# First loads of an attention-and-rational-FFN kernel: S2 leads ScalarE's queue, the first keys go in two halves over two queues, and the written-out order is replaced

## The chip, the cores and the metric

One core of a Trainium2 chip runs the whole kernel. The metric is the device time of one launch in microseconds; the median of three runs before the change is 265.93 us (265.91 to 265.98). Differences are told as time after over time before.

## What is computed

Two parts follow each other. The first is attention with polynomial sketch features: for each of 4 batches and 4 heads, 1088 rows of q and k (32 wide) are multiplied by two small matrices S1 and S2 (8 x 32 each), and the 8 x 8 products of the two results are the 64 features of a row. Keys' features are summed against v (and against ones, for the denominator); a query's output is its features times that sum, divided by the denominator. The second part is a feed-forward layer whose activation is a ratio of polynomials.

```python
def phi(x):
    a = np.einsum('rd,bhsd->bhsr', S1, x)
    b = np.einsum('rd,bhsd->bhsr', S2, x)
    return np.einsum('bhsi,bhsj->bhsij', a, b).reshape(*x.shape[:-1], r * r)
q_p, k_p = (phi(q), phi(k))
kv = np.einsum('bhsf,bhsd->bhfd', k_p, v)
z = np.sum(k_p, axis=2)
num = np.einsum('bhsf,bhfd->bhsd', q_p, kv)
den = np.einsum('bhsf,bhf->bhs', q_p, z)[..., None] + 1e-06
...
h = x @ w_in                       # x: 4352 x 128, w_in: 128 x 2048
P = a[0] + a[1] * h + a[2] * h2 + a[3] * h3
Q = 1.0 + np.abs(b[0]) * np.abs(h) + np.abs(b[1]) * h2
g = P / (Q + 1e-06)
return (g @ w_out).astype(np.float32)
```

S1, S2, the four numbers a and the two numbers b are inputs like the rest, in DRAM at launch.

## The kernel before

**The order is written out by hand.** The kernel lists its work as steps: `step(engine, ..., fn, ...)` appends one, in the order of the source, and only notes which buffers it uses. Step number n of that list is emitted at position `PLACE[n]`. Each engine runs its own steps in that order and waits, by semaphores, for whatever a step needs; nothing overtakes on an engine or on its DMA queue. The numbers for cost, rank and slack that the calls carry (among them `GET_SLACK` and `S_SLACK`) are not used when the kernel is emitted. `ON_ACT` lists the steps that may run on either of two engines and are given to ScalarE; the rest of those go to VectorE. `FILLS` gives positions ahead of which TensorE runs multiplications of a zero tile (L321), so many each; they compute nothing that is used. `FILL = 1` adds one at the very start.

**The loads.** `dma(...)` issues one transfer, from SyncE's queue (SP) or from ScalarE's (ACT). All lines of it are L268. At the start SP issues S1, S2, the first 256 columns of q of batch 0 (`q0_a`), v of batch 0 in two parts (`load_v`, by partitions 0 to 63 and 64 to 127), then half of w_out, the rest of q0 (`q0_b`), the keys of batch 1, the other half of w_out and the first half of w_in. ScalarE issues the keys of batch 0 in one transfer of 544 KB (`load_k`, 128 partitions of 4352 bytes), then b, loads its activation table, and issues a. S1 and S2 land in 8 rows each of one tile, `s_raw`.

**The start.** VectorE copies `s_raw` four times side by side into `s_rep` (L352). TensorE transposes that (L349), and VectorE multiplies it with masks into `S12` (L355, for keys) and two tiles `SAB` (L362, for queries); GpSimd copies it once more for later queries. Keys of batch 0: VectorE transposes them in 32 x 32 blocks into `kT` (L415, L417), in two pieces, tiles 0 to 3 and 4 to 8. In five parts (`K0_PARTS`: tile 0, tiles 1 to 3, 4 and 5, 6 and 7, 8) TensorE makes the sketches (L435), ScalarE copies one half (L440), VectorE multiplies the halves into features `k_p` (L443) and TensorE multiplies them with v (L454). ScalarE copies the sum into `kvz` (L473). Queries: block transposes (L498), two sketches (L520), a copy on ScalarE (L528 or L525), the product on VectorE (L535 or L532), then the multiplication with `kvz` (L589), the division (L598, L602, L605), a transpose on TensorE (L611) and a copy into `xT` (L618). Later groups of queries go through DRAM: a smaller sketch (L548), a copy (L553), two transfers out (`put`), three back (`get`), a product (L556).

**w_out.** The kernel needs w_out in bfloat16, five times: as it is and scaled with each of a's four numbers; each is made in two halves from the raw load (L391, L393 on ScalarE, L395, L397 on VectorE). Six of these ten steps are on ScalarE.

**The feed-forward part** runs in 29 units. A unit is up to six blocks of 512 rows by 128 columns of the hidden layer (the first four and the last ones are smaller). `hidden` multiplies (L691), ScalarE copies to bfloat16 (L695), VectorE and ScalarE make the ratio in passes: the absolute value (L706), b's polynomial (L711 or L713, then L716), its reciprocal as Ln and Exp on ScalarE (L719, L722), powers of h times that reciprocal (L726 to L752), and `gather` multiplies the results with the copies of w_out (L787). The string `MODES` has one digit a unit. A mode tells how a's polynomial is shared out: in mode 4 the powers go to TensorE one by one, four multiplications a block; in mode 3 a pass a3*h + a2 is made on VectorE or ScalarE (L726 or L728) and three multiplications a block remain; in mode 2 two. Finished columns are transposed by VectorE (L799) and written out (L811).

Of the kernel before, what the change touches and what calls it, by code (L numbers as in the profile page):

```python
# [20 lines left out]
def kernel(  # L21
# [103 lines left out]
    def d_four(n, ptr):  # L125
# [20 lines left out]
    GET_SLACK = 1.2  # L146
    S_SLACK = (0.0, 1.0)
# [5 lines left out]
    MODES = '43242333333243333233444244424'  # L153
# [60 lines left out]
    )  # L214
    ON_ACT = (
        25, 26, 29, 31, 32, 33, 328, 342, 344, 379, 454, 478, 502, 535, 612, 636, 669, 688, 693, 744, 878,
        889, 914, 932, 951, 953, 960,
    )
    FILLS = {7: 15, 22: 4, 70: 1, 77: 1}
    NW = 5 if '4' in MODES else 3  # L220


# [643 lines left out]
```

## Time and profile before

| what | value |
|---|---|
| median of 3 runs | 265.93 us (265.91 to 265.98) |
| the profiled execution, time and span | 265.84 us, 264.1 us |
| granted clock of TensorE | 1.00 |
| VectorE's first instruction | 4.34 us after the span's start |
| ScalarE's first instruction after its table load | 6.18 us |
| first hidden matmul (L691) | 16.53 us |
| last instruction that computes (VectorE, L799) | 260.24 us, 0.45 us long |
| bytes moved by DMA | 20.13 MB, mean 76 GB/s |

The span runs from the first to the last recorded instruction; the time is that of the launch and is 1.8 us longer. The costliest lines are L691 (127.2 us of TensorE, 320 matmuls), L787 (97.8 us of TensorE, 480), the copies L695 (69.4 us of ScalarE), Ln and Exp (65.5 and 65.4 us of ScalarE) and the two products L716 and L731 (40.4 us of VectorE each). In the lists that follow, a row of a timeline has the start, the time taken, the engine (ACTq and SPq are the queues that issue DMAs), the line, the operation with output and input, and the count; in brackets stands the idle time before it and what ended it. A row of waits has the engine and the work that waited, what it waited for, the total in us, how often and the longest.

### The profile page before, as it was taken

Reading aid. Unit: us, or ns where it says so; the run is one execution under the profiler, and the core shown is the slowest. Engines: PE = TensorE matmul, PEld = TensorE weight load, DVE = VectorE, ACT = ScalarE, POOL = GpSimd, SP = SyncE. Lnnn points to the kernel's source line nnn. Section 1 sums busy time; section 2 is a strip of 40 time slices with the busy share of each in tenths; the row PEclk is TensorE's granted clock in tenths of the full one; section 3 lists DMA queues with packets and bytes.
Section 4 is the critical chain, followed back from the end, with each engine's and each line's share of the span. In section 5 each row is a group of like instructions: output and inputs, shape, how many; then the busy total and the mean of one; then the engine's idle time right before and its main releaser. Section 6 shows DMA issues by size and latency. Waiting matters only on the chain.

```text
span 264.1 us, 4201 instructions
## 1 busy us (share of the span) xinstructions
PE 254.8 (96%) x1641; PEld 141.1 (53%) x1659; DVE 252.4 (96%) x293; ACT 248.5 (94%) x209; POOL 2.7 (1%) x25
## 2 busy tenths in 40 slices
PE   8999999999999999999999999999999999999994
PEld 5767646554544654454444554444444466565683
DVE  3889999999999999999999999999999999999994
ACT  2779999999999999999999999999999999999991
POOL 4000000000000000000000000000000000000000
PEclk9999999999999999999999999999999999999999
DMA  7969344800425347005102530300010110030032
GB/s 199 338 193 241 79 134 128 242 32 0 97 70 178 93 132 163 4 7 129 34 2 80 104 87 21 55 0 0 0 22 2 25 18 0 0 46 0 0 55 40
DMA packets 29063, 20.13 MB, mean 76 GB/s; under 512 B 19316, under 2 KB 24948, under 8 KB 29044
## 3 DMA queue, kind: packets, MB, share of 16 engines
q1 hardware_dynamic: 28352, 19.24, 29.2%
q10 hardware_dynamic: 692, 0.62, 0.8%
q8 instruction: 13, 0.21, 0.4%
q14 instruction: 6, 0.05, 0.1%
HBM read 16.65 MB, written 3.21 MB: 75 GB/s over the span
## 4 chain that ended last, share of the span: by engine, by line
ACT 51%; PE 30%; DVE 10%; issue 8%; POOL 0%; ACTq 0%; POOLq 0%
PE h_ps L691 14%; ACT ln L719 13%; ACT t L722 13%; ACT t L695 11%; PE out_ps L787 7%; ACT t L728 6%; ACT t L713 3%; DVE t L734 2%; DVE t L737 2%; PE att_ps L589 1%; DVE t L731 1%; PE att_ps L548 1%; DVE t L716 1%; PE att_ps L321 1%; PE att_ps L435 1%
## 5 line engine op out<-in xcount | busy, mean ns | idle before, releaser
L691 PE MATMUL h_ps<-xT,w_in_sb 128*128 128x512 f32 (+1 forms) x320 | 127.2, 534 | 1.2 <-ACT xT L618 0.7
L787 PE MATMUL out_ps<-t,w_out 128*128 128x512 bf16 (+1 forms) x480 | 97.8, 344 | 1.9 <-issue 1.1
L691 PEld LDWEIGHTS h_ps<-xT,w_in_sb 128*128 128x128 f32 x320 | 58.8, 190 | 45.4 <-issue 33.3
L787 PEld LDWEIGHTS <-w_out 128*128 128x128 bf16 x498 | 47.2, 98 | 49.5 <-issue 17.9
L695 ACT CAST t<-h_ps 128x1024 bf16<-128x1024 f32 (+1 forms) x69 | 69.4, 1053 | 0.5 <-PE h_ps L691 0.4
L719 ACT ACTIVATE ln<-t 128x3072 f32<-128x3072 bf16 (+4 forms) x29 | 65.5, 2257 | 0.3 <-DVE t L716 0.2
L722 ACT ACTIVATE t<-ln 128x3072 bf16<-128x3072 f32 (+4 forms) x29 | 65.4, 2254 | 0.2
L731 DVE TENSOR_TENSOR t<-t,t 128x3072 bf16<-128x3072 bf16 (+4 forms) x29 | 40.4, 1397 | 0.0
L716 DVE TENSOR_TENSOR t<-t,t 128x3072 bf16<-128x3072 bf16 (+4 forms) x29 | 40.4, 1392 | 0.0
L728 ACT ACTIVATE t<-t,a_sb 128x3072 bf16<-128x3072 bf16 (+2 forms) x13 | 33.3, 2574 | 0.4 <-PE out_ps L787 0.4
L734 DVE TENSOR_TENSOR t<-t,t 128x3072 bf16<-128x3072 bf16 (+3 forms) x23 | 32.7, 1425 | 0.1
L706 DVE TENSOR_SCALAR t<-t 128x3072 uint16<-128x3072 uint16 (+4 forms) x29 | 22.4, 773 | 0.6 <-ACT t L695 0.4
L711 DVE TENSOR_SCALAR t<-t,b_abs 128x3072 bf16<-128x3072 bf16 (+3 forms) x24 | 22.3, 928 | 0.0
L737 DVE TENSOR_TENSOR t<-t,t 128x3072 bf16<-128x3072 bf16 (+1 forms) x13 | 21.6, 1661 | 0.0
L589 PEld LDWEIGHTS att_ps<-kvz,a_all 128*64 128x64 f32 x288 | 9.9, 137 | 4.2 <-issue 2.3
L589 PE MATMUL att_ps<-kvz,a_all 128*64 128x66 f32 x288 | 11.3, 225 | 0.0
L752 DVE TENSOR_TENSOR t<-t,t 128x1024 bf16<-128x1024 bf16 (+3 forms) x10 | 11.2, 1124 | 0.0
L556 DVE TENSOR_TENSOR a_all<-a_all,b_all 128x768 f32<-128x768 f32 (+2 forms) x11 | 9.6, 871 | 0.0
L713 ACT ACTIVATE t<-t,b_abs 128x2048 bf16<-128x2048 bf16 (+3 forms) x5 | 9.0, 1809 | 0.1
L443 DVE TENSOR_TENSOR k_p<-att_ps,b_sk 128x768 f32<-128x768 f32 x9 | 8.5, 949 | 0.0
L454 PEld LDWEIGHTS att_ps<-v_sb,k_p 128*64 128x64 f32 x216 | 6.8, 138 | 2.1 <-issue 1.4
L740 DVE TENSOR_TENSOR t<-t,t 128x3072 bf16<-128x3072 bf16 (+3 forms) x6 | 7.7, 1282 | 0.0
(75 smaller groups left out, 145.9 us busy)
## 6 DMA issues: line engine op xcount, KB each, us to landing
a_all<-sk_d SPq DMA_DIRECT2D x6, 384.0 KB
b_all<-sk_d SPq DMA_DIRECT2D x12, 192.0 KB
kq<-in_k_dram SPq DMA_DIRECT2D x3, 544.0 KB
kq<-in_q_dram SPq DMA_DIRECT2D x3, 544.0 KB
a_all<-sk_d SPq DMA_DIRECT2D x4, 320.0 KB
b_all<-sk_d SPq DMA_DIRECT2D x8, 160.0 KB
v_sb<-in_v_dram SPq DMA_DIRECT2D x4, 288.0 KB
v_sb<-in_v_dram SPq DMA_DIRECT2D x4, 256.0 KB
```

The costliest lines, as they stand in the source:

```text
L589: nc.tensor.matmul(nd.t[x:x + 64, o:o + 2 * KW], lhsT=(av(c)[:, o0 + x:o0 + x + 64] if how == "direct" else q_p.t[:, c * n + o0 + x:c * n ...
L691: nc.tensor.matmul(h.t[:, cols[x] - cols[x0]:cols[x + 1] - cols[x0]], lhsT=w_in_sb[:, f * 128:(f + 1) * 128], rhs=xT[:, xpos(t0):xpos(t0) ...
L695: nc.scalar.copy(out=hh.t[:, cols[x0]:cols[x1]], in_=h.t[:, 0:cols[x1] - cols[x0]])
L706: nc.vector.tensor_scalar(out=u.t[:, :n].bitcast(U16), in0=hh.t[:, :n].bitcast(U16), scalar1=0x7FFF, scalar2=None, op0=AX.bitwise_and)
L716: nc.vector.tensor_mul(out=y.t[:, :n], in0=w.t[:, :n], in1=u.t[:, :n])
L719: nc.scalar.activation(out=ln.t[:, :n], in_=y.t[:, :n], func=ACT.Ln, bias=1.0 + 1e-6)
L722: nc.scalar.activation(out=r.t[:, :n], in_=ln.t[:, :n], func=ACT.Exp, scale=-1.0)
L728: nc.scalar.activation(out=p.t[:, :n], in_=hh.t[:, :n], func=ACT.Identity, scale=a3, bias=a2)
L731: nc.vector.tensor_mul(out=s.t[:, :n], in0=hh.t[:, :n], in1=r.t[:, :n])
L734: nc.vector.tensor_mul(out=(hh if mode == 3 else p).t[:, :n], in0=hh.t[:, :n], in1=s.t[:, :n])
L737: nc.vector.tensor_mul(out=hh.t[:, :n], in0=p.t[:, :n], in1=hh.t[:, :n])
L787: nc.tensor.matmul(o[0].t[:, :bl[x][1]], lhsT=w_sb[y_][:, bl[x][2], :], rhs=src.t[:, cols[x]:cols[x + 1]], start=(o[1] == 1), stop=(o[1] = ...
```

## The change

Four things change in the code.

1. S2 is issued by ScalarE, as the first of its queue, rather than by SyncE behind S1.
2. The keys of batch 0 are two transfers: partitions 0 to 63 by ScalarE behind S2, partitions 64 to 127 by SyncE behind S1.
3. The last unit (256 rows by 128 columns) goes from mode 4 to mode 3. That takes one of its four matmuls L787 away, and adds one pass of 256 columns a partition, given to ScalarE (step 966 of `ON_ACT`).
4. `PLACE`, `ON_ACT` and `FILLS` are new. There is one step more (977). The two numbers for slack have no part in what is emitted.

The head of each list, read from the two tables (numbers in brackets are warming matmuls in front):

| | before | after |
|---|---|---|
| SP queue | S1, S2, q0_a, v, v, w_out 2nd half, q0_b, keys of batch 1, w_out 1st half, w_in 1st half | S1, keys 64-127, q0_a, v, v, w_out 2nd half, q0_b, w_out 1st half, keys of batch 1, w_in 1st half |
| ACT queue | keys, b, table, a | S2, keys 0-63, b, a, table |
| VectorE | s_rep, kT of tiles 0-3, S12, SAB, qT, SAB, kT of tiles 4-8, features of tile 0, 1-3, query product, features 4-5, 6-7, 8 | s_rep, SAB, S12, SAB, kT of tiles 0-3, qT, kT of tiles 4-8, features of tile 0, 1-3, 4-5, query product, features 6-7, 8 |
| TensorE | (1+15) L349, (4) L435 of tile 0, 1-3, L377, L520, L520, L435 of 4-5, 6-7, L454 of tile 0, 1-3, L435 of 8, L454 of 4-5, 6-7, 8 | (1+9) L349, (8) L435 of tiles 1-3, tile 0, L520, L435 of 4-5, L520, L435 of 8, L454 of tile 0, L435 of 6-7, L377, L454 of 1-3, 4-5, 6-7, 8 |
| ScalarE, from its fifth copy L440 to L473 | a part of w_out ahead of it, one behind it | two parts of w_out behind it |

Of the w_out steps, ScalarE had the second halves of the copies 0, 2 and 3, the first half of copy 1 and both of copy 4; it now has both of 0 and 2 and the second of 1 and 4. In the rest of the kernel the steps of every engine keep their engine and mostly their neighbourhood, but 312 of TensorE's 354 have another rank than before, 193 of VectorE's 286 and 182 of ScalarE's 209.

```diff
     FILL = 1
     LATE = 6.96
     Q0B_RANK = -194.15
-    GET_SLACK = 1.2
-    S_SLACK = (0.0, 1.0)
+    GET_SLACK = 1.1
+    S_SLACK = (0.0, 0.0)
     V_SLACK = 0.99
     GAP = 0.2
     START = 4.9
     Q0_PRE = -151.2
     K1_RANK = 0.47
-    MODES = '43242333333243333233444244424'
+    MODES = '43242333333243333233444244423'
     FIRST_PER = 4
     LAST_PER = (8, 8, 8, 4, 3, 1)
     K0_PARTS = ((0, 1), (1, 4), (4, 6), (6, 8), (8, 9))
@@ -163,60 +163,60 @@
     PERS = (6,)
     N_T = 16
     PLACE = (
-        0, 3, 1, 8, 4, 5, 10, 2, 9, 18, 13, 71, 16, 17, 11, 6, 7, 14, 19, 21, 15, 29, 33, 30, 80, 46, 91,
-        66, 83, 58, 111, 43, 90, 101, 12, 24, 22, 23, 25, 38, 26, 27, 28, 39, 36, 40, 42, 48, 37, 41, 47,
...
+        1, 0, 3, 7, 6, 8, 9, 10, 4, 5, 27, 20, 65, 26, 21, 11, 2, 12, 14, 13, 16, 15, 42, 43, 60, 97, 57,
+        63, 46, 78, 45, 93, 103, 72, 79, 17, 25, 22, 28, 29, 37, 18, 19, 30, 47, 31, 32, 33, 48, 38, 39, 41,
...
     )
     ON_ACT = (
-        25, 26, 29, 31, 32, 33, 328, 342, 344, 379, 454, 478, 502, 535, 612, 636, 669, 688, 693, 744, 878,
-        889, 914, 932, 951, 953, 960,
+        25, 26, 28, 29, 30, 34, 329, 343, 345, 380, 455, 479, 503, 536, 613, 637, 670, 689, 694, 745, 879,
+        890, 915, 933, 952, 954, 961, 966,
     )
-    FILLS = {7: 15, 22: 4, 70: 1, 77: 1}
+    FILLS = {12: 9, 18: 8, 76: 1, 80: 1}
     NW = 5 if '4' in MODES else 3
 
 
@@ -263,10 +263,11 @@
 
     k0, q0, v0 = Buf("kq"), Buf("kq"), Buf("v_sb")
 
-    def dma(out_, in_, rank, mbytes, after=(), uses=(), eng=SP, early=0.0, rate=300, cost=0.46, slack=0.3, behind=None):
+    def dma(out_, in_, rank, mbytes, after=(), uses=(), eng=SP, early=0.0, rate=300, cost=0.46, slack=0.3, behind=None, name="go"):
         def go():
             (nc.sync if eng == SP else nc.scalar).dma_start(out=out_() if callable(out_) else out_,
                                                             in_=in_() if callable(in_) else in_)
+        go.__name__ = name
         return step(eng, cost, go, rank, after=after, uses=uses, land=mbytes * 1e3 / rate, early=early,
                     slack=slack, behind=behind)
 
@@ -288,11 +289,12 @@
         return dma(s_raw[i * R:(i + 1) * R], s_in, rank, 0.001, eng=eng, cost=0.4, slack=S_SLACK[i], behind=behind)
 
     s_l = [load_s(0, -206, SP)]
-    s_l.append(load_s(1, -205.9, SP, behind=s_l[0]))
+    s_l.append(load_s(1, -208, ACTE))
     FIRST = 256
-    k0_l = load_k(0, k0, -207, slack=0.15, rate=420, eng=ACTE)
+    k0_l = [dma(lambda x=x: k0.t[x:x + 64], flat(k, 0)[x:x + 64], -207 + 0.01 * x, 0.279, (), [k0], rate=420, slack=0.15,
+                eng=(ACTE, SP)[x // 64], behind=s_l[1 - x // 64], name=("go", "half")[x // 64]) for x in (0, 64)]
     table = step(ACTE, 1.3, lambda: nc.scalar.preload_act_table_set("natural_log_exp_and_others"), -205, behind=k0_l[0])
-    q0_a = dma(lambda: q0.t[:, 0:FIRST], flat(q, 0)[:, 0:FIRST], -203.8, 0.131, (), [q0], rate=350, slack=0.2, behind=s_l[1])
+    q0_a = dma(lambda: q0.t[:, 0:FIRST], flat(q, 0)[:, 0:FIRST], -203.8, 0.131, (), [q0], rate=350, slack=0.2, behind=k0_l[1])
     v0_l = load_v(0, v0, -203.7, slack=0.4, rates=(340, 205), behind=q0_a)
     ab_in = []
     for c, w, x in ((4, 2, moe_b), (0, 4, moe_a)):

```

Line numbers from here on are those of the kernel before; after the change, lines from L268 on stand one or two further down.

92 rows, old and new, of the table PLACE are left out of this document.

## The prediction

> **What bounds the kernel now.** I read the busy table of the page first, then busy time by stretch, then the waits of the first 28 us, then the start in order of time.
>
> ```profile
> PE 254.8 (96%) x1641; PEld 141.1 (53%) x1659; DVE 252.4 (96%) x293; ACT 248.5 (94%) x209; POOL 2.7 (1%) x25
> ```
>
> ```profile
> 12.00:16.00 4.00, 3.38 (x43) 1.94 (x41) 3.00 (x7) 2.61 (x8) 0.00 (x0) 1.00 0.71 202
> 16.00:20.00 4.00, 4.00 (x33) 3.47 (x30) 3.56 (x13) 3.62 (x6) 0.00 (x0) 1.00 0.73 230
> 20.00:250.00 230.00, 227.04 (x1349) 119.77 (x1366) 228.73 (x238) 229.07 (x176) 0.00 (x0) 1.00 0.26 64
> ```
>
> Columns of the second fence: stretch, its length, busy us of TensorE, weight loads, VectorE, ScalarE, GpSimd; granted clock, DMA share, GB/s. From 20 to 250 us three engines are busy at once: VectorE is idle 1.27 us, ScalarE 0.93 us, TensorE 2.96 us. No single engine can be relieved there; an order can only lose or save that little, and the start (idle VectorE, ScalarE) is where time lies.
>
> ```profile
> DVE s_rep L352 <- DMA s_raw<-in_S_dram: 4.3, 1, 4.3
> ACT b_sk L440 <- PE h_ps L435: 3.2, 2, 3.1
> DVE a_all L535 <- PE att_ps L520: 0.5, 1, 0.5
> ```
>
> ```profile
> 0.73 0.39 ACTq L268 DMA_DIRECT2D kq<-in_k_dram  x1
> 0.73 0.74 SPq L268 DMA_DIRECT2D s_raw<-in_S_dram  x2
> 4.34 0.21 DVE L352 COPY s_rep<-s_raw 16x128 f32<-16x128 f32 x1 [4.34 <-DMA s_raw<-in_S_dram]
> 4.49 0.41 SPq L268 DMA_DIRECT2D ln<-in_moe_w_out_dram  x1
> 4.49 0.77 DVE L415 STREAM_TRANSPOSE kT<-kq 128x256 f32<-128x256 f32 x2
> 5.19 0.19 DVE L355 TENSOR_TENSOR S<-att_ps,mask 128x64 f32<-128x64 f32 x1
> 5.30 0.28 DVE L362 TENSOR_TENSOR SAB<-att_ps,mask 128x128 f32<-128x128 f32 x1
> 5.50 0.43 DVE L498 STREAM_TRANSPOSE qT<-kq 128x256 f32<-128x256 f32 x1
> 5.84 0.25 DVE L362 TENSOR_TENSOR SAB<-att_ps,mask 128x128 f32<-128x128 f32 x1
> 6.02 0.75 DVE L415 STREAM_TRANSPOSE kT<-kq 128x256 f32<-128x256 f32 x2
> 11.92 0.43 ACT L473 COPY kvz<-out_ps 64x66 f32<-64x66 f32 x2
> 16.53 1.99 PE L691 MATMUL h_ps<-xT,w_in_sb 128*128 128x256 f32 x8
> ```
>
> Here: start, us, engine, work. VectorE waits 4.34 us for the two little matrices. The trace's packet records say why: S1's eight packets run at 1.68 to 1.76 us, S2's at 3.40 to 3.66, behind the keys' 128 packets (from 1.79; 0.17 us each once running; the last ends at 4.11). S1's semaphore is full at 2.10 us, S2's at 4.25, the keys' at 4.47.
>
> **S2 first on ScalarE's queue.** It leaves at 0.73 us like S1, with nothing in front, so I take S1's 2.10 us for it. s_rep then runs at 2.2. TensorE's warming matmuls (L321) ahead of the transpose L349 fall from 16 to 10, 0.213 us apart from 1.29: they end near 3.3. From L349 to S12 it is 0.48 us (4.70 to 5.19), so the three mask products run from 3.8 to 4.4, before the keys. Their room behind the keys was 0.11 + 0.20 + 0.18 us, start to start (5.19 to 5.30, 5.30 to 5.50, 5.84 to 6.02): **-0.49 us** of VectorE. s_rep itself gives nothing: its end was the keys' landing anyway.
>
> **Keys in two halves.** Both leave second on their queues, near 1.15 us (S2's old issue was at 1.19), not at 0.73: 0.39 to 0.46 us late. S1 and S2 bring 16 packets of 0.013 us, nothing. The halves need the same 128 packets on the same engines, which in the old load were full from 2.5 us. Bounds for the landing: 4.47 (two issuers fill the 16 engines at once; before, the first 0.5 us had them 3 of 16 busy) to 4.47 + 0.39 = 4.86. I take 4.75, nearer the late end as the engines, not the queue, were full: **+0.28 us** (0 to 0.39). The transposes need all partitions, so both halves count. The SP queue gets a 64-row issue in S2's place, so q0's and v's issues stay near 1.5 and 1.9; on ScalarE's queue b, a and the table load (1.28 us) follow, done by 4 us, before its first use at 6.18.
>
> The Trainium skill, "DMA: Bandwidth & Descriptors" (Rules for kernel authors), says of two transfers to disjoint partition halves: "Don't bother", they share the same engines and serialize. The trace agrees as far as S2's packets waited for the keys' to end. By that rule the split alone gains nothing and the landing is at 4.86; the sum would be 0.1 us worse.
>
> **The waiting queue.** In the trace the ninth load on, each issue waits on the semaphore of an earlier load: w_out's first half left at 4.49 us, when the keys had landed. One more load stands in front now, and an early S load is the one waited for, so this issue can go at about 3.3, right after v (2.71 + 0.61). It fills a hole at 6.5 to 7.0 us (11 engines busy, else 17): about 0.2 us less. Against the 0.39 late start all loads land 0.2 us later or less; w_in's first half, full at 16.02 us, lands near 16.2. w_out's second issue goes ahead of the next batch's keys, which are used at 18.0 us against 11.83 landed, so cost nothing.
>
> **The order up to the first hidden matmul.** TensorE now has the sketches L435 of tiles 4 and 5 ahead of the second L520 pair, and VectorE their features ahead of the query's. VectorE's gap of 0.55 (8.07 to 8.62) and 0.15 us before 9.53 can close: 0 to -0.70. But TensorE's products L454 (72 at 0.035 us, 2.5 us) then come late in one row, and ScalarE has two w_out parts (1.05 + 1.16 us, startable at w_out's landing, 9.34 + 0.2) ahead of kvz L473, that is 11.7 against 11.92. So I keep less than half: **-0.3 us**. Eight fills later on replace four: they fall in the wait for the keys; without that cover 4 x 0.213 = 0.85 us.
>
> **w_out parts.** Six on ScalarE and four on VectorE as before; both casts now on ScalarE (1.05 against 1.15) and a scale for a cast on VectorE (0.73 against 0.68): -0.1 and +0.05 us, within rounding.
>
> **Last unit, mode 4 to 3.** One matmul L787 fewer (0.11 us), one ScalarE pass of 256 more: bounds 0.35 (the 256-wide L695) and 0.42 (L719). ScalarE has 6.1 idle us after 250; it now ends a_exp near 257.9, VectorE uses it at 258.6. VectorE's last three products (0.28 each), which end the kernel, stay. 0; without that cover +0.4.
>
> **Everything later** is permuted: of 354 TensorE steps 312 have another rank. Taken at 0; bounded by the idle above: -0.9 (ScalarE's) to +1.7 (below).
>
> Sum: -0.49 + 0.28 - 0.3 = -0.5 us. It is made against the profiled execution, 265.84 us with a span of 264.1, 1.8 us outside it; the median shown is 0.1 higher, 265.93. Forecast **265.4**. A difference of 0.2%, 0.53 us, is what I count as told from no change: 265.40 to 266.46.
>
> **Rivals.**
> (1) *The loads hold the start.* The first hidden matmul needs w_in's first half whole. 16.2 + 0.1 against 16.53 leaves 0.2 us of gain, however early the keys are: **265.7**. For it: landing and use are only 0.5 us apart. Against: VectorE keeps its 0.49 us lighter and has other work.
> (2) *All of it arrives.* Keys at 4.47 and both gaps closed: -0.49 - 0.70 = -1.2: **264.7**. Against: ScalarE's kvz place.
> (3) *Slower: halves at a 64-partition rate.* The load of v to the upper 64 partitions moves 1152 B in 0.083 us, 13.9 GB/s an engine, the keys 25.6. At that rate a key packet takes 0.31 us, eight in a row 2.5 against 1.36: keys +1.1, plus 0.39, less 0.49: +1.0, and w_in 1.3 late, which agrees: **266.9**. It decides once a packet takes over 0.25 us. Against: v's lower half runs at 0.046 us for 1024 B, 22 GB/s, and the two halves run side by side. "SBUF — State Buffer" of the Trainium skill (Can I just issue two DMAs to hit both halves?) says two such loads gained only 6% over one; no run here shows it yet.
> (4) *Slower: tight handoffs.* The Ln L719 has no ScalarE step between it and the product L716 it needs in 16 of 29 units, before in 9. The wait that the trace shows for such a pair is 0.24 us (251.09, on VectorE L716). Seven more: +1.7 less 0.5: **267.1**; it decides from three of them. Against: place alone does not say that VectorE is late.
>
> **How the numbers follow.** Chances: forecast 0.36 (own range 265.05 to 265.75, half on each side of 265.40), (1) 0.20, (2) 0.17, (3) 0.11, (4) 0.16. Faster: 0.17 + 0.18 + 0.03 = 0.38; the same: 0.18 + 0.17 = 0.35; slower 0.27. The range goes from (2) to (3), 264.7 to 266.9; it leaves out parts of (2) and (4).
>
> **What would show it.** s_rep at 2.2 us and the mask products before 4.5; the first key transpose at 4.75 (at 5.9 for rival 3, with packets of 0.3 us); w_out's first issue at 3.3; no VectorE wait on L520; kvz near 11.7; the first L691 near 16.2 (at w_in's landing for rival 1). For rival 4 ScalarE's idle from 20 to 250 us grows past 2 us with Ln waiting for L716. I am wrong if keys land after 5.2, or if the first L691 comes later than 16.5.

## The result and the profile after

| | before | after |
|---|---|---|
| median of 6 runs on the same chip | 265.96 us (265.51 to 266.20) | 270.46 us (268.44 to 271.14) |
| ratio, 95% interval | | 1.0148 [1.0125, 1.0171] |
| the profiled execution, time and span | 265.84, 264.1 us | 269.98, 268.2 us |

The kernel became slower by 4.5 us, and its runs spread over 2.7 us where those of before spread over 0.7. From here on lines after L268 have the numbers of the kernel after: two more than in the kernel before.

The busy table of after, then busy time by stretch (stretch, its length, TensorE, weight loads, VectorE, ScalarE, GpSimd, granted clock, DMA share, GB/s):

```profile
PE 259.6 (97%) x1656; PEld 142.1 (53%) x1656; DVE 252.8 (94%) x293; ACT 249.0 (93%) x210; POOL 2.7 (1%) x25
...
8.00:12.00 4.00, 4.00 (x36) 2.46 (x34) 2.54 (x6) 1.26 (x5) 0.00 (x0) 1.00 1.15 297
...
20.00:250.00 230.00, 229.02 (x1365) 119.27 (x1362) 228.20 (x244) 228.60 (x178) 0.00 (x0) 1.00 0.28 67
```

One of the same stretches of before:

```profile
8.00:12.00 4.00, 4.00 (x100) 3.54 (x100) 3.22 (x8) 2.85 (x8) 0.00 (x0) 1.00 1.08 364
```

From 20 to 250 us ScalarE is idle 1.40 us (before 0.93), VectorE 1.80 (1.27), TensorE 0.98 (2.96): that part did not change. From 8 to 12 us TensorE is busy all the time in both, but before it worked off 100 instructions and after 36. Either it has other instructions, or each one takes longer; the start in order of time says which.

The waits of after in the first 28 us (engine, work, what it waited for, total us, times, longest), then its start in order of time:

```profile
DVE s_rep L354 <- DMA s_raw<-in_S_dram: 2.3, 1, 2.3
DVE kT L417 <- DMA kq<-in_k_dram: 2.1, 1, 2.1
...
PE h_ps L437 <- DVE kT L417: 1.5, 1, 1.5
```

```profile
0.73 0.60 ACTq L268 DMA_DIRECT2D s_raw<-in_S_dram  x1
...
1.19 0.57 SPq L268 DMA_DIRECT2D kq<-in_k_dram  x1
1.36 0.52 ACTq L268 DMA_DIRECT2D kq<-in_k_dram  x1
1.81 0.58 SPq L268 DMA_DIRECT2D kq<-in_q_dram  x1
...
3.56 1.89 PE L323 MATMUL out_ps<-idle 128*128 128x256 bf16 x8
3.73 0.29 DVE L364 TENSOR_TENSOR SAB<-att_ps,mask 128x128 f32<-128x128 f32 x1 [1.23 <-PE att_ps L351]
3.79 0.60 SPq L268 DMA_DIRECT2D ln<-in_moe_w_out_dram  x1
...
6.44 0.77 DVE L417 STREAM_TRANSPOSE kT<-kq 128x256 f32<-128x256 f32 x2 [2.08 <-DMA kq<-in_k_dram]
6.94 1.44 PE L437 MATMUL h_ps<-S,kT 128*64 128x64 f32 x16 [1.49 <-DVE kT L417]
...
8.31 1.23 PE L522 MATMUL att_ps<-qT,SAB 64*128 64x256 f32 x4
9.46 0.69 PE L437 MATMUL out_ps<-S,kT 128*64 128x64 f32 x8
...
15.68 0.43 ACT L475 COPY kvz<-out_ps 64x66 f32<-64x66 f32 x2 [0.30 <-PE out_ps L456]
20.45 0.48 PE L693 MATMUL h_ps<-xT,w_in_sb 128*128 128x256 f32 x1
```

The same TensorE work in the kernel before:

```profile
5.80 0.69 PE L435 MATMUL h_ps<-S,kT 128*64 128x64 f32 x16
6.73 0.70 PE L520 MATMUL att_ps<-qT,SAB 64*128 64x256 f32 x4
8.79 0.45 PE L435 MATMUL out_ps<-S,kT 128*64 128x64 f32 x8
```

S came early (s_rep waits 2.3 us and not 4.3) and VectorE then stands still for 2.08 us until the keys are there. TensorE has worked off its eight fills by 5.45 and stands still for 1.49 us. And what it does then takes longer piece by piece: 16 key sketches 1.44 us against 0.69, four query sketches 1.23 against 0.70, eight key sketches 0.69 against 0.45. In the trace's records the matmuls of the key sketches come in close pairs; a pair starts 0.106 us after the one in front of it, where before it is 0.058 us, and this lasts until about 14 us. The column of the granted clock says 1.00 in every one of these stretches; it does not show this.

The loss, by four points that both profiles have:

| stretch | before, us | after, us | difference |
|---|---|---|---|
| start to first key transpose | 4.49 | 6.44 | +1.95 |
| to kvz | 7.43 | 9.24 | +1.81 |
| to the first hidden matmul | 4.61 | 4.77 | +0.16 |
| to the end of the last computing instruction | 244.16 | 244.26 | +0.10 |
| sum | 260.69 | 264.71 | +4.02 |

So the 244 us for which most of the order was rewritten cost 0.1 us more, and the loss lies in the first 16 us.

### The profile page after: what moved, and what is told of

Its sections match the earlier page's. It is cut to its first block, busy times and chain, and to the rows that moved or that the text cites. A ratio compares the mean times of both kernels' runs of the same rounds, so it can differ in the third digit from the quotient of the medians.

```text
span 268.2 us, 4222 instructions
## 1 busy us (share of the span) xinstructions
PE 259.6 (97%) x1656; PEld 142.1 (53%) x1656; DVE 252.8 (94%) x293; ACT 249.0 (93%) x210; POOL 2.7 (1%) x25
## 4 chain that ended last, share of the span: by engine, by line
PE 60%; ACT 20%; DVE 11%; issue 5%; DMA 2%; ACTq 0%; DVEq 0%
PE h_ps L693 30%; PE out_ps L789 16%; ACT ln L721 6%; ACT t L697 6%; ACT t L724 4%; DVE t L754 3%; PE att_ps L591 3%; PE att_ps L456 3%; DVE t L733 2%; ACT t L730 2%; DMA kq<-in_k_dram 2%; PE att_ps L437 2%; PE att_ps L550 2%; DVE t L718 1%; DVE t L736 1%
## 5 line engine op out<-in xcount | busy, mean ns | idle before, releaser
L789 PE MATMUL out_ps<-t,w_out 128*128 128x512 bf16 (+1 forms) x497 | 101.6, 346 | 0.2
L697 ACT CAST t<-h_ps 128x1024 bf16<-128x1024 f32 (+2 forms) x69 | 70.0, 1049 | 1.0 <-PE h_ps L693 0.9
L730 ACT ACTIVATE t<-t,a_sb 128x3072 bf16<-128x3072 bf16 (+3 forms) x14 | 34.1, 2438 | 0.0
L736 DVE TENSOR_TENSOR t<-t,t 128x3072 bf16<-128x3072 bf16 (+3 forms) x23 | 32.6, 1426 | 0.0
L739 DVE TENSOR_TENSOR t<-t,t 128x3072 bf16<-128x3072 bf16 (+2 forms) x14 | 21.9, 1562 | 0.0
L754 DVE TENSOR_TENSOR t<-t,t 128x1024 bf16<-128x1024 bf16 (+2 forms) x9 | 10.9, 1221 | 0.0
L456 PE MATMUL att_ps<-v_sb,k_p 128*64 128x64 f32 x216 | 7.8, 225 | 0.0
```

Source lines behind the costliest of these rows:

```text
L456: nc.tensor.matmul(kv.t[p0:p0 + 64, c0:c0 + 64].rearrange("p (n d) -> p n d", d=D), lhsT=k_p.t[:, t - t0, h].rearrange("p i j -> p (i j)") ...
L697: nc.scalar.copy(out=hh.t[:, cols[x0]:cols[x1]], in_=h.t[:, 0:cols[x1] - cols[x0]])
L730: nc.scalar.activation(out=p.t[:, :n], in_=hh.t[:, :n], func=ACT.Identity, scale=a3, bias=a2)
L736: nc.vector.tensor_mul(out=(hh if mode == 3 else p).t[:, :n], in0=hh.t[:, :n], in1=s.t[:, :n])
L789: nc.tensor.matmul(o[0].t[:, :bl[x][1]], lhsT=w_sb[y_][:, bl[x][2], :], rhs=src.t[:, cols[x]:cols[x + 1]], start=(o[1] == 1), stop=(o[1] = ...
```

## The experiments

The theories, as the expectations name them. **A**: the keys' division by partitions is the loss (later also: with what TensorE does in the longer pause). **B**: the new order loses by itself. **C**: two queues moving large loads at once are the loss, however they are divided. **D**: TensorE runs at half its pace because of the pause in front of its first sketches (a pause is filled or made by the number of fills, so the runs can't tell its length from a lack of work ahead of the sketches). **E**: the spread of the runs comes from the loads. A ratio is the estimate on record with its interval, not the quotient of the medians. The last three columns are from one profiled execution each, in us: two starts and their distance. In whole, b_split and b_s2 that execution is at the low end of the range.

| run | time, median (range) | ratio, interval | key transpose | kvz | between |
|---|---|---|---|---|---|
| after | 270.46 (268.44 to 271.14) | 1.0148 [1.0125, 1.0171] | 6.44 | 15.68 | 9.24 |
| whole | 267.94 (266.28 to 270.82) | 1.0096 [1.0046, 1.0147] | 5.75 | 12.12 | 6.37 |
| cols | 266.61 (266.09 to 267.76) | 1.0020 [1.0002, 1.0038] | 5.15 | 12.11 | 6.96 |
| warm | 267.57 (267.36 to 267.66) | 1.0046 [1.0031, 1.0061] | 6.50 | 13.08 | 6.58 |
| b_split | 269.33 (267.13 to 269.65) | 1.0103 [1.0069, 1.0137] | 5.62 | 13.16 | 7.54 |
| whole_warm | 266.29 (266.14 to 266.74) | 1.0009 [0.9999, 1.0018] | 5.64 | 12.15 | 6.51 |
| b_s2 | 268.00 (266.52 to 269.63) | 1.0062 [1.0033, 1.0092] | 5.66 | 12.71 | 7.05 |
| b_cold | 268.72 (268.25 to 269.27) | 1.0094 [1.0075, 1.0114] | 4.75 | 15.30 | 10.55 |
| a_first | 266.93 (266.57 to 271.44) | 1.0031 [1.0020, 1.0042] | 5.59 | 12.78 | 7.19 |
| sp_keys | 266.32 (266.04 to 266.70) | 0.9991 [0.9959, 1.0023] | 5.34 | 12.53 | 7.19 |
| old_loads | 266.19 (266.01 to 267.03) | 0.9989 [0.9953, 1.0026] | 5.57 | 11.93 | 6.36 |
| mix | 265.87 (265.39 to 266.69) | 0.9998 [0.9984, 1.0011] | 4.51 | 11.67 | 7.16 |

In the same columns the kernel before has 4.49, 11.92 and 7.43. From the first hidden matmul to TensorE's end all of them, before and after too, take 243.65 to 243.78 us.

### whole: after, with the keys as one transfer behind S2 on ScalarE's queue

```diff
-    k0_l = [dma(lambda x=x: k0.t[x:x + 64], flat(k, 0)[x:x + 64], ...
+    k0_l = load_k(0, k0, -207, slack=0.15, rate=420, eng=ACTE, behind=s_l[1])
```

> The changed kernel with the keys of batch 0 as one transfer of 128 partitions, second on ScalarE's queue behind S2; order, S2, warming matmuls and last unit as changed. Theory A (the division by partitions is the loss: the halves land at 6.4 us, TensorE falls idle and then runs at half rate): the keys land at 4.7 to 5.1, the first key sketches run at the old pace (16 records in 0.7 us), the first hidden matmul comes at 16 to 17 us and the time is 265 to 266.5. Theory B (the new order loses by itself): keys early, but still over 268.

The keys' packets are back at 0.168 us, and the key transpose starts at 5.75: 0.7 us earlier, not the 1.9 that would undo the whole delay. The median is above the 265 to 266.5 that A expected. In the profiled execution (266.28) TensorE's later pieces have the short times again, but the runs range from 266.28 to 270.82. B is out for the later 244 us. What holds the keys still: ScalarE's first issue took 0.60 us, so the keys' began at 1.36, and the packets of q0, which SyncE had issued at 1.19, ran ahead of them (from 2.19; the keys' 2.72 to 5.02).

### cols: after, with the keys divided by columns

```diff
-    k0_l = [dma(lambda x=x: k0.t[x:x + 64], flat(k, 0)[x:x + 64], ... for x in (0, 64)]
+    k0_l = [dma(lambda x=x: k0.t[:, x:x + 544], flat(k, 0)[:, x:x + 544], ... for x in (0, 544)]
```

> The changed kernel with the keys divided by columns: each queue moves 128 partitions of 2176 bytes. Theory A: both halves land near 5 us, time 265 to 267 as with one transfer. Theory C (two queues at once are the loss, however the keys are divided): landing at 6 us or later, time as the changed kernel, 269 to 271.

Timeline of this kernel:

```profile
1.19 0.37 SPq L268 DMA_DIRECT2D kq<-in_k_dram  x1
...
1.36 0.36 ACTq L268 DMA_DIRECT2D kq<-in_k_dram  x1
...
5.15 0.77 DVE L417 STREAM_TRANSPOSE kT<-kq 128x256 f32<-128x256 f32 x2 [0.77 <-DMA kq<-in_k_dram]
...
5.65 1.44 PE L437 MATMUL h_ps<-S,kT 128*64 128x64 f32 x16 [0.18 <-DVE kT L417]
...
7.72 0.45 PE L437 MATMUL out_ps<-S,kT 128*64 128x64 f32 x8
```

The same two queues, the same bytes, issued at the same times, and the keys are used 1.29 us earlier: only the division differs. C falls. A packet of 2176 bytes took 0.088 us, 24.7 GB/s for one DMA engine, close to the 25.9 of the undivided load (4352 bytes in 0.168). TensorE's pause shrinks to 0.18 us; its first 16 sketches still take 1.44 us; the next key sketches have the short time.

### b_split: the kernel before, with its keys in two halves by partitions

```diff
-    k0_l = load_k(0, k0, -207, slack=0.15, rate=420, eng=ACTE)
+    k0_l = [step(ACTE, 0.46, lambda: nc.scalar.dma_start(out=k0.t[0:64], in_=flat(k, 0)[0:64]), -207, uses=[k0])]
...
+        nc.sync.dma_start(out=k0.t[64:128], in_=flat(k, 0)[64:128])
         nc.sync.dma_start(out=q0.t[:, 0:FIRST], in_=flat(q, 0)[:, 0:FIRST])
```

> The kernel before with the keys divided by partitions alone: 0 to 63 first on ScalarE's queue, 64 to 127 on SyncE's behind S1 and S2. Theory A: the keys land 1.5 to 2 us later than 4.47, and the time is 267.5 to 270. Theory B: within 0.5 us of before.

With nothing else of the change the keys are used 1.13 us later (5.62) and the kernel is slower. They land at 5.53, 1.06 us later than before and not the 1.5 to 2 that A expected. ScalarE's half, which started first, had 0.168 us a packet, SyncE's half behind it 0.291. SyncE's half is third on its queue here, so this run doesn't tell the division from the place; cols does. The profiled execution is the fastest of five (267.13) and has the short times of TensorE; the other four took 269.27 to 269.65, and no trace shows why.

The key packets, from the trace's packet records. A load's semaphore is full when 16 increments have come; the last column counts those that had come when the load's last packet ended:

```
kernel   part of the keys    first start  last end  median us  semaphore full  last end to full  in by last end
before   whole, ScalarE      1.79         4.11      0.168      4.47            0.36              15
after    64 rows, SyncE      2.54         4.09      0.230      4.96            0.87              0
after    64 rows, ScalarE    3.44         5.27      0.280      6.41            1.14              0
cols     columns, SyncE      2.18         4.04      0.088      4.39            0.35              12
cols     columns, ScalarE    3.12         4.77      0.088      5.13            0.36              12
b_split  64 rows, ScalarE    2.08         3.47      0.168      4.36            0.89              0
b_split  64 rows, SyncE      3.10         4.67      0.291      5.53            0.86              0
whole    whole, ScalarE      2.72         5.02      0.168      5.73            0.71              15
b_s2     whole, ScalarE      2.60         4.91      0.168      5.63            0.72              10
sp_keys  whole, SyncE        2.18         4.86      0.168      5.32            0.46              14
```

(Packets of 4352 bytes, in cols of 2176.) The two parts of a divided load overlap by 0.4 to 0.9 us and otherwise run one after the other. What marks the division by partitions is, first, the packets once the first half is gone: in after 0.20 to 0.34 us from 4.2 us on, with a median of 0.30, that is 13 to 22 GB/s for an engine. And second the end: a half counts as landed 0.86 to 1.14 us after its last packet, when none of the 16 increments had come; a load over all 128 partitions 0.35 to 0.72 us after it, with ten or more of the 16 in. The delay of 1.94 us in landing (4.47 to 6.41) is then 0.75 for the first packet (1.79 to 2.54), 0.41 for the packets' run (2.32 to 2.73 us from first to last) and 0.78 from last packet to landing (0.36 to 1.14). The Trainium skill, "SBUF — State Buffer" (Can I just issue two DMAs to hit both halves?), says that two transfers on partitions 0 and 64 gain only 6% over a single one and serialize, and that it takes one transfer over all 128 partitions to reach all ports. In outcome the runs agree: halves land at 6.41, parts over all partitions at 5.13 with the same issues.

### warm: after, with eight more fills in the pause

```diff
-    FILLS = {12: 9, 18: 8, 76: 1, 80: 1}
+    FILLS = {12: 9, 18: 16, 76: 1, 80: 1}
```

> The changed kernel with 16 warming matmuls in place of 8 between the transpose of S1 and S2 and the first key sketches, which covers TensorE until the keys land at 6.4 us. If TensorE's half rate from 6.9 to about 13 us is worth what it seems (sketches 1.44 against 0.69 us, the two query sketches 1.23 against 0.70 each), the sketches take 0.7 us again and the time falls by 1.5 to 2 us, to 268.5; if the late keys alone make the loss, it stays at 270 to 270.5.

Timeline of this kernel:

```profile
3.56 2.54 PE L323 MATMUL out_ps<-idle 128*128 128x256 bf16 x16
...
7.00 1.01 PE L437 MATMUL h_ps<-S,kT 128*64 128x64 f32 x16 [0.90 <-DVE kT L417]
7.93 0.70 PE L522 MATMUL att_ps<-qT,SAB 64*128 64x256 f32 x4
```

Work that computes nothing made the kernel 2.9 us faster (270.46 to 267.57; 1.5 to 2 were expected), with the keys as late as in after (6.50). The pieces have the short times, and four runs lie within 0.3 us. The fills themselves show the change of pace: in the records they start 0.213 us apart as in after, and from 4.95 us on 0.109 us apart. From key transpose to kvz it takes 6.58 us, not 9.24: **2.66 us** is what the half pace costs. D holds: with work in the pause the half pace is gone, though 0.90 us of pause are left. Here the hidden part met another limit: its first weight load waited 0.3 us for w_in, which became full at 18.0 us.

### whole_warm: whole, with three more fills

```diff
-    FILLS = {12: 9, 18: 8, 76: 1, 80: 1}
+    FILLS = {12: 9, 18: 11, 76: 1, 80: 1}
```

> One transfer of the keys behind S2 (as in whole) and 11 warming matmuls in place of 8 ahead of the first key sketches, so that TensorE has no pause before them. whole ran from 266.3 to 270.8 us. Theory D (an execution's loss beyond the late keys is TensorE at half rate, entered through the pause): every execution within 0.5 us of 266.2, ratio 1.000 to 1.002. Theory E (the spread comes from the loads): the spread stays 2 us or more.

Against whole the profiled execution is the same (12.12 and 12.15 for kvz), but the median falls from 267.94 to 266.29 and ten runs lie within 0.6 us. The loads are the same, so that they don't make the spread: E falls. That TensorE's pace made it is inferred, since no slower execution of whole was profiled. With the keys whole and the pace kept the rest of the change is at 1.0009.

### b_cold: the kernel before, with fewer fills

```diff
-    FILLS = {7: 15, 22: 4, 70: 1, 77: 1}
+    FILLS = {7: 7, 22: 1, 70: 1, 77: 1}
```

> The kernel before with 7 and 1 warming matmuls in place of 15 and 4; loads and order untouched, so keys still land at 4.5 us. Theory D: the sketches run at half pace (about 0.11 us a pair in place of 0.058) and the time is 267 to 270, with a spread of 1 us or more. If TensorE's pace does not hang on what it did before, the time stays within 0.3 us of before.

Timeline of this kernel:

```profile
4.83 0.26 PE L349 MATMUL att_ps<-ident,s_rep 16*128 16x16 f32 x1 [1.84 <-DVE s_rep L352]
...
5.68 1.12 PE L435 MATMUL h_ps<-S,kT 128*64 128x64 f32 x16 [0.28 <-DVE S L355]
...
7.26 1.23 PE L520 MATMUL att_ps<-qT,SAB 64*128 64x256 f32 x4
```

Old loads and old order, a pause of 1.84 us in TensorE: the long times appear, key transpose to kvz goes from 7.43 to 10.55 us and the kernel is 2.6 us slower. The effect needs nothing of the change: fewer fills, with the pause that they leave, are enough.

### b_s2: the kernel before, with S2 ahead of the whole keys on ScalarE's queue

```diff
-    s_l.append(load_s(1, -205.9, SP, behind=s_l[0]))
+    s_l.append(load_s(1, -208, ACTE))
```

(With the places of these first steps exchanged so that the queue has that order.)

> The kernel before with S2 issued by ScalarE ahead of the keys, keys whole, order else as before. If the keys' place on the queue is the price (whole: first key transpose at 5.75 against 4.49 us), the keys are used at 5.7 again, the first hidden matmul comes 0.8 to 1.2 us later and the time is 266.8 to 267.2, with a spread if TensorE pauses. If the late keys of whole came from the new order, they land at 4.5 to 4.9 here and the time is within 0.4 us of before.

S2's 1 KB in front cost the keys 1.17 us (5.66 against 4.49), and the earlier masks gave back 0.38 (7.05 between, against 7.43). So that part of the change alone is a loss. TensorE waits 1.11 us before its sketches here and keeps the short times in the profiled execution (its fills are 0.109 us apart before the wait); the runs spread from 266.5 to 269.6, and the median is above the 266.8 to 267.2 expected.

### a_first: after, with S2 and S1 on SyncE's queue and the whole keys behind a on ScalarE's

```diff
-    s_l.append(load_s(1, -208, ACTE))
+    s_l.append(load_s(1, -208, SP))
...
-    for c, w, x in ((4, 2, moe_b), (0, 4, moe_a)):
+    for c, w, x in ((0, 4, moe_a), (4, 2, moe_b)):
```

> The changed kernel with S2 and S1 both on SyncE's queue and the keys as one transfer on ScalarE's queue behind the short load of a alone (b behind the keys), 10 warming matmuls. From key transpose to first hidden matmul the new order takes 11.1 us (whole), the old one 12.0. If the keys are used by 5.0 and S2 is there before them, the first hidden matmul comes at 16.1 and the time is 265.5, better than before; if S2 falls behind the keys' packets again, VectorE has the mask products behind the keys and the time is 266 to 267.

With a's 16 bytes and not S2 ahead, the keys are used at 5.59, about as late. It is the second place on the queue that costs, not what S2 is. S2 was there early (s_rep starts at 2.58), so neither case of the expectation came. ScalarE then waits 0.36 us for w_out ahead of kvz.

### sp_keys: after, with the keys whole and second on SyncE's queue

```diff
+    k0_l += load_k(0, k0, -206, slack=0.15, rate=420, eng=SP, behind=s_l[0])
```

> The kernel after, but with the first keys as one transfer of 128 partitions, second on SyncE's queue behind S1; S2 stays alone at the head of ScalarE's queue, with b and a behind it; q0 follows the keys on SyncE's queue; nine early fills in place of eight. Theory A (the division by partitions and what TensorE does in the longer pause are the whole loss; the new order by itself saves about 0.9 us from the first key transpose to the first hidden matmul): nothing runs ahead of the keys any more but S1, so the packets take 0.17 us each, the first key transpose starts at 4.7 to 5.1, the sketches' first records lie 0.46 us apart, the first hidden matmul starts at 15.9 to 16.3 and the time is 265.2 to 265.8, ratio 0.997 to 0.999. Rival (a load issued second on a queue comes late wherever it is): the first key transpose at 5.5 or later, the first hidden matmul at 16.7 or later, 266.2 or more. Theory B (the new order loses by itself) expects over 268 with either.

The keys are used at 5.34, later than the bound that theory A gave, with q0 and v queued behind and only S1 ahead. The first hidden matmul at 17.28 and the median are where the rival put them (16.7 or later, 266.2 or more); its key transpose, at 5.5 or later, came a little earlier. The keys' packets run from 2.18 to 4.86 against 1.79 to 4.11: 0.39 later at the start and 0.75 at the end. The expectation of 0.997 to 0.999 failed; the interval does not tell this kernel from before. It is wide since runs of before on that chip lay high too, six of 23 at 268.9 to 270.9; no trace shows what these lost.

### old_loads and mix: the new order with the old loads

```diff
-    s_l.append(load_s(1, -208, ACTE))
+    s_l.append(load_s(1, -208, SP))
...
+    k0_l = load_k(0, k0, -207, slack=0.15, rate=420, eng=ACTE)
...
-    FILLS = {12: 9, 18: 8, 76: 1, 80: 1}
+    FILLS = {12: 15, 18: 6, 76: 1, 80: 1}
```

> The kernel after with its order, but with the loads of the kernel before: S2 and S1 on SyncE's queue, the first keys whole and first on ScalarE's. The keys land at 4.5 as before, but VectorE's list has the mask products ahead of the key transpose, and they need S, so that this can't begin before the products are done. Theory A (the order is sound, the loads are the loss): first key transpose at 5.3 to 5.6, first hidden matmul at 16.5 to 16.9, time 265.9 to 266.4, ratio 1.000 to 1.002. Theory B (the order loses by itself, in the 250 us behind): 269 to 271, as the kernel after. The fills are set so that none stands for long between the key sketches and the keys.

It came as theory A expected: key transpose 5.57, first hidden matmul 16.68, median 266.19. The keys were there at 4.66, but VectorE's list has the masks first and they need S. mix puts the key transposes ahead of the masks again (four entries of the list of places exchanged, four fills in the wait and not six):

> The kernel after with the loads of the kernel before (as in the run with its order and the old loads), and on VectorE the first key transposes ahead of the mask products again, as the kernel before has them; six early fills in the wait become four. Theory A (what the loads cost was the whole loss; the order behind the keys is worth something if the keys start as early as before): first key transpose at 4.5, the mask products in the transposes' shade as before, first sketches 0.46 us apart, first hidden matmul at 16.0 to 16.3, time 265.4 to 265.8 where the kernel before is at 266.0, ratio 0.997 to 0.999. Rival (the order gives its 0.9 us only where the masks are done ahead of the keys, so that it is worth nothing with the old loads): first hidden matmul at 16.5 or later, 266.0 or more.

Timeline of mix:

```profile
4.51 0.75 DVE L417 STREAM_TRANSPOSE kT<-kq 128x256 f32<-128x256 f32 x2
...
9.67 1.06 ACT L395 CAST w_out<-ln 128x1024 bf16<-128x1024 f32 x1
10.62 1.16 ACT L393 ACTIVATE w_out<-ln,a_sb 128x1024 bf16<-128x1024 f32 x1
...
11.67 0.42 ACT L475 COPY kvz<-out_ps 64x66 f32<-64x66 f32 x2
...
16.42 1.99 PE L693 MATMUL h_ps<-xT,w_in_sb 128*128 128x256 f32 x8
```

The first hidden matmul starts 0.11 us earlier than before (16.53), not the 0.2 to 0.5 expected, and the time is that of before, 0.9998 [0.9984, 1.0011]. So the rival's reading is nearer: with the old loads the order is worth about nothing. kvz comes two w_out parts after the first of them starts (2.00 us; 2.00 or 2.01 in whole, cols, old_loads, sp_keys and a_first), and the products that it reads end only 0.15 us before it. No version that was run beats the kernel before.

## Why the prediction was wrong

**S2 first on ScalarE's queue: right in itself.** s_rep at 2.29 (2.2 foretold), masks at 3.73 to 4.35 (3.8 to 4.4). The 0.49 us that it was to save is 0.38 in b_s2. (In the kernel before S2's packets, at 3.40 to 3.66, came behind most of the keys' packets, not behind their end at 4.11.) What the prediction did not see is its price: the issue of 1 KB in front held up the whole keys by 1.17 us in b_s2.

**Keys in two halves: this step failed.** It put the landing between 4.47 and 4.86 and took +0.28 us; the keys landed at 6.41, +1.94. It reasoned that the halves need the same 128 packets on the same engines and so the same time, and counted only the later issue. Its first packet came 0.75 us later and not 0.39: the issue began 0.46 us later, it took 0.57 us and not 0.39, and 0.11 is not explained. The packets took 0.41 longer and the landing behind the last of them 0.78 longer, both counted as nothing. cols splits it by cause: 0.66 us for two queues and the second place on them (4.49 to 5.15), 1.29 for the division by partitions (5.15 to 6.44). Rival (3) came nearest: it foretold packets of 0.31 us from v's upper half, and the later half has 0.28. But it took this for all packets (+1.1 us), and b_split's first half alone ran at 0.168, so that the packets cost 0.41 in all; it lacked the late landing, its keys at 5.9 were still 0.5 early, and it was given 0.11.

**The fills: the second step that failed.** "Eight fills later on replace four: they fall in the wait for the keys; without that cover 4 x 0.213 = 0.85 us" priced fills that are too many. Here they were too few: they ended at 5.45, the keys came a microsecond later, and the pause of 1.49 us cost 2.66 us in the work behind it, by warm. TensorE's pace was taken as given. No rival had it, though the trace of before has both paces: its fills at the start are 0.213 us apart, and behind the same fill at 15.18 us the next matmul starts after 0.12:

```profile
15.18 0.28 PE L321 MATMUL out_ps<-idle 128*128 128x256 bf16 x1
...
15.30 0.38 PE L611 MATMUL att_ps<-ident,x_tok 128*128 128x128 f32 x2
```

The range's upper end, 266.9, lacked this term.

**The order up to the first hidden matmul.** -0.3 us was taken, -0.1 is what mix shows. VectorE's gap in front of the query's features closes in mix (L537 starts at 8.91 without a wait), and as the prediction feared the gain stays in ScalarE's two w_out parts ahead of kvz. In after itself kvz is at 15.68, not 11.7.

**The waiting queue.** w_out's first issue left at 3.79, not 3.3, since the two issues ahead of it took 0.57 and 0.58 us. w_in's first half was full at 16.5 in after and used at 20.45, so rival (1) is out there; in warm alone it decides, by 0.3 us.

**w_out parts, last unit, everything later: right in sum.** All together 0.1 us over 244 us; no run takes them apart. Rival (4), tight handoffs, is out: ScalarE's idle time from 20 to 250 us is 1.40 us where it was to pass 2. Rival (2) had the keys at 4.47, which did not happen.

The text's own test, "wrong if keys land after 5.2, or if the first L691 comes later than 16.5", says so on both counts: 6.41 and 20.45. In sums: 1.95 of delay, 2.66 of pace, -0.85 from the early masks and the order (warm's 6.58 against 7.43 of before), 0.26 behind, make the 4.02 us.

**What stays open.** Why the second place on a queue costs 0.85 to 1.26 us, more than the 0.46 to 0.63 by which the issue is later: in whole and b_s2 q0's packets that ran ahead may be part of it, and so is the last of the 16 increments (0.71 and 0.72 us after the last packet, against 0.36 before); in sp_keys the last packets came late, and no run says why. Why a half counts as landed so long after its last packet, and why only the later half's packets are slow. And what decides TensorE's pace: the length of the pause alone does not. In whole the half pace of the fills lasts to the pause of 0.81 us, and the sketches behind it soon run at the full one; in cols the pause is 0.18 us, and the half pace lasts until about 7.4 us.

## What to carry to other kernels

A load that is to be shared between two queues is divided by columns, with all 128 partitions in each part, though here no divided load landed as early as the whole one at the head of its queue (5.13 against 4.47); and a small transfer put in front of a large one costs the large one far more than its bytes. When a load moves, look at what TensorE does until it lands: a pause right after the warming multiplications is priced by the whole stretch of matmuls behind it, not by its own length, and a few more multiplications of zeros in it cost next to nothing. A profile shows this as busy time with fewer instructions in it; compare the distance of equal matmuls, since the busy share and the granted clock look healthy.

## What the runs showed of the hardware

- TensorE at half its pace for some 7 us while the granted clock stands at 1.00: pairs of equal matmuls 0.106 us apart against 0.058. It followed a pause of 1.49 us in after and one of 1.84 in b_cold; in both the fills ahead of the pause were still 0.213 us apart, where in warm they come 0.109 us apart from 4.95 us on. The Trainium skill, "TensorE: Matmul & The Clock Gate" (Part 1: The HAM clock gate), describes two rates, one half of the other, a window of about 3.4 us for going down and for going up, and one that runs freely, so that runs of one kernel differ. The two rates agree, and runs that differ (whole, 266.28 to 270.82) fit; the pauses here are shorter than that window, and came before TensorE had run at the full pace. It calls the ramp less than 1% of a typical span; the 2.66 us that warm took away are 0.99% of 268.2.
- A load in two halves of 64 partitions was slow at its end: the packets of the later half took 0.20 to 0.34 us (after, from 4.2 us on), against 0.168 for those of b_split's first half while it ran alone and for a whole load. A half's semaphore was full 0.86 to 1.14 us after its last packet, against 0.35 to 0.72 for loads of the keys over all partitions.
- The first issue on ScalarE's queue took 0.60 us when it was S2 (1 KB) and 0.54 when it was a (16 bytes), against 0.39 for the keys' 544 KB. On this queue a short transfer was no shorter issue; as the first on SyncE's, S1, which is as small as S2, took 0.39.
